# Attention tails of 64 queries as fp32 quarters of the array, in a fused retention, mixture-of-attention and token-mixing kernel

## The chip, the cores and the metric

One core of one Trainium2 chip runs the whole kernel. The metric is the device time of one execution in microseconds; lower is better. The time before the change is 927.81 us, the median of three runs (925.51 to 928.01).

## The reference

Three layers follow one another, on 8 batches of 576 positions. The first is a retention layer with 8 heads of 64. Its output x (512 wide) goes to four attention experts, and theirs to a token and channel mixing. The change touches the second layer only:

```python
logits = x @ w_gate                      # 4 experts, the best 2 count
topk = np.argpartition(-logits, K, axis=-1)[..., :K]
...
for e in range(E):
    q = x @ wq[e]
    k = x @ wk[e]
    v = x @ wv[e]
    scores = scale * (q @ k.transpose(0, 2, 1))
    scores = np.where(causal, -1000000000.0, scores)
    scores = scores - scores.max(-1, keepdims=True)
    a = np.exp(scores)
    a /= a.sum(-1, keepdims=True) + 1e-09
    ye = a @ v @ wo[e]
    for kk in range(K):
        mask = topk[:, :, kk] == e
        out += mask[..., None] * w[:, :, kk:kk + 1] * ye
```

All inputs and outputs are fp32.

## The kernel before, in words

**Attention units.** The 576 queries of a batch are four chunks of 128 and a tail of 64. The four experts are handled as two pairs (p = 0, 1). A unit (b, p, m) is query chunk m of one pair, for both experts of the pair (s = 0, 1). Its keys are those up to its own chunk; for the tail, m = 4, all 576. There are 80 units, of which 16 are tails.

**Precision.** Most products are made of operands split into a high and a low fp32r part (`split`, lines 102 and 103: a ScalarE copy and a VectorE subtraction), three matmuls each (`mm3`, lines 97 to 99). `proj_qk` makes Q and K of a pair that way, in two halves of 288 columns (g = 0, 1). For the scores, U holds Q's high and low part on the two halves of the partitions, and KK holds K's high part on both halves and K's low part on both halves; four DMAs per half of K, on SyncE's queue, copy KN into KK (line 225).

**One unit.** `at_scores` makes the scores in two matmuls per expert (line 309). VectorE adds the causal mask and takes the row minimum of the negated scores in one operation (line 312, two instructions: the operation and a read of its accumulator). ScalarE does the exponential with the row sum (line 317, again with a read of the accumulator). The tail's 576 keys don't fit one PSUM bank, so it has two parts of 288 and eight matmuls, and its second reduction starts from the first one's minimum. `at_trans` transposes P in blocks on TensorE with an identity (line 356); VectorE copies expert 0's blocks to PT and ScalarE expert 1's (lines 361 and 363). For the tail these are five blocks per expert, of 64 columns. `at_out` multiplies by V (line 375), for the query chunks (0), (1, 2) and (3, 4) together; key chunk 4 of V has 64 rows. `at_norm` turns the row sums of a pair into weights (lines 325 to 331).

**fp32 products** without a split (lines 132, 154, 161, 173 and 375) are two instructions each in the trace. Those of the retention scores (`ret_scores`, line 132) and its state (`ret_state`, line 173) use 64 rows and 64 columns, a quarter of the array.

**What sets the order.** TensorE's order is that of the program. VectorE, ScalarE and GpSimd take their instructions in an order that is made at build time, and each runs its queue in that order. At step t the program issues the scores of unit t, then projections by a table of slots, then the transposes of unit t-1, then retention work of the next batch and the products with V:

```python
SLOTS = [("Q01 K10", "R0"), ("", ""), ("K11 Q10", ""), ("Q11", "R1"), ("", "R2"),
         ("v0", "R3"), ("v1", ""), ("v2 k00", "R4"), ("q00", "R5"), ("v3 k01 v4 g", "")]
```

The first pair's tail is step 4 of a batch, between the retention steps R1 and R3. The second pair's is step 9, ahead of the projections v3, k01 and v4. Retention masks are VectorE's (lines 138 and 141), as are the gated outputs xt (line 181), which ScalarE and GpSimd split (lines 183 and 184). The last batch has no retention to do for a next one; token tiles fill its steps.

**Beside this**, about one job a step converts 64-bit weights to fp32r pairs (lines 434 to 455: SyncE loads, VectorE, ScalarE and GpSimd work), queued behind the step's reductions and exponentials (MARK). The PSUM pool has seven working banks ("w"), and P has five buffers.

## Time and profile before

| What | Value |
|---|---|
| Median of three runs | 927.81 us |
| Lowest and highest run | 925.51 and 928.01 us |
| The profiled execution, its own time | 925.94 us |
| Its span, from first to last instruction | 924.2 us |
| Mean granted TensorE clock | 0.991 |
| Matmul instructions | 8526 |

The span is what the trace shows; the 1.7 us beside it lie around the first and last instruction. Matmuls are pipelined, so the time from one start to the next is shorter than the duration of one, and a group of them is read by the start of what follows. PE is TensorE's matmul, PEld its weight load, DVE VectorE, ACT ScalarE, POOL GpSimd, SP SyncE.

### The profile page before, as it was taken

The numbers are of one execution on the slowest core, as the hardware profiler recorded it, in microseconds if no ns is written. First come the engines' busy times: TensorE is split into PE (matmuls) and PEld (weight loads), VectorE is DVE, ScalarE is ACT, GpSimd is POOL, SyncE is SP. The second block draws the span as 40 slices with busy tenths as digits, with TensorE's granted clock in tenths as the row PEclk, the third lists the DMA queues.
The fourth block names the chain that finished last, engine by engine and source line by source line (L and its number), as shares of the span: only waits on it lengthen the run. The fifth ranks groups of instructions, "written<-read, shape, count | busy, mean of one in ns | idle before, by whom it ended". The sixth has DMA issues, their size and how long they took to land.

```text
span 924.2 us, 22725 instructions
## 1 busy us (share of the span) xinstructions
PE 887.6 (96%) x8526; PEld 817.3 (88%) x8526; DVE 661.9 (72%) x2003; ACT 440.4 (48%) x1166; POOL 223.8 (24%) x276
## 2 busy tenths in 40 slices
PE   7899989999999999999999899999999999999998
PEld 6788978888888888888878899999999999999998
DVE  6487776877879787787777976766668674777632
ACT  2265645556556555555666533434334432444320
POOL 4316153361534525243121102102020110101010
PEclk8999999999999999999999899999999999999999
DMA  8667665776666776655685442343513333151311
GB/s 308 198 165 211 174 182 159 199 211 177 197 185 176 230 192 198 166 163 141 192 276 192 126 93 65 70 115 87 145 33 76 90 79 90 27 135 24 92 34 52
DMA packets 146205, 132.27 MB, mean 143 GB/s; under 512 B 83376, under 2 KB 121648, under 8 KB 146096
## 3 DMA queue, kind: packets, MB, share of 16 engines
q1 hardware_dynamic: 145952, 130.55, 50.5%
q8 instruction: 67, 1.10, 0.5%
q0 software_dynamic: 144, 0.28, 0.2%
q14 instruction: 42, 0.34, 0.1%
HBM read 80.20 MB, written 32.00 MB: 121 GB/s over the span
## 4 chain that ended last, share of the span: by engine, by line
PE 55%; DVE 7%; DMA 4%; ACT 3%; issue 2%; SPq 1%; POOL 1%; ACTq 0%; DVEq 0%; POOLq 0%
PE acc L712 22%; PE w L97 8%; PE w L99 8%; PE w L98 8%; PE w L375 3%; PE w L247 2%; PE w L309 2%; DMA KK<-KN 1%; ACT P L317 1%; DVE sm L138 1%; PE w L356 1%; DMA wost<-wot 1%; DMA og<-gd 1%; PE w L132 1%; DVE cs L577 1%
## 5 line engine op out<-in xcount | busy, mean ns | idle before, releaser
L712 PE MATMUL acc<-TK,zh 128*128 128x256 f32 (+1 forms) x1024 | 181.4, 300 | 3.9 <-DVE u L726 3.2
L712 PEld LDWEIGHTS acc<-TK,zh 128*128 128x128 f32 x1024 | 156.2, 192 | 4.5 <-ACT cs L575 3.4
L317 ACT ACTIVATE P<-P,st 128x128 f32<-128x128 f32 (+4 forms) x160 | 95.7, 600 | 68.0 <-DVE st L312 67.6
L712 PE MATMUL acc<-TK,zl 128*128 128x256 f32 (+1 forms) x512 | 110.7, 298 | 0.0
L728 POOL TENSOR_TENSOR ul<-u,uh 128x576 fp32r<-128x576 f32 x16 | 24.3, 1541 | 324.2 <-ACT uh L727 237.0
L712 PEld LDWEIGHTS acc<-TK,zl 128*128 128x128 f32 x512 | 87.4, 192 | 0.0
L102 ACT ACTIVATE zh<-cs 128x512 fp32r<-128x512 f32 x64 | 40.3, 631 | 90.1 <-PE acc L712 70.6
L375 PE MATMUL w<-PT,V 128*64 128x192 f32 (+3 forms) x576 | 67.1, 329 | 14.5 <-DVE PT L361 8.1
L97 PE MATMUL w<-xh,WH 128*128 128x288 f32 x256 | 76.6, 299 | 2.9 <-DVE sm L141 2.6
L103 DVE TENSOR_TENSOR zl<-cs,zh 128x512 fp32r<-128x512 f32 x64 | 44.9, 706 | 48.0 <-ACT zh L102 46.4
L309 PE MATMUL w<-KK,U 128*64 128x288 f32 (+4 forms) x384 | 77.8, 329 | 0.9 <-DMA KK<-KN 0.9
L575 ACT ACTIVATE cs<-cs 128x512 f32<-128x512 f32 x72 | 45.1, 631 | 67.4 <-DVE cs L573 54.0
L98 PE MATMUL w<-ul,CH 128*128 128x256 f32 (+1 forms) x256 | 75.7, 296 | 0.0
L375 PEld LDWEIGHTS w<-PT,V 128*64 128x64 f32 (+1 forms) x576 | 43.0, 138 | 36.9 <-ACT PT L361 13.2
L99 PE MATMUL w<-uh,CH 128*128 128x256 f32 (+1 forms) x256 | 75.7, 296 | 0.0
L97 PE MATMUL w<-uh,CH 128*128 128x256 f32 (+1 forms) x256 | 75.5, 297 | 0.1
L98 PE MATMUL w<-xl,WH 128*128 128x288 f32 x256 | 75.3, 294 | 0.0
L99 PE MATMUL w<-xh,WL 128*128 128x288 f32 x256 | 75.3, 294 | 0.0
L312 DVE CUSTOM_DVE_ANT_0 P<-w,cm 128x128 f32<-128x128 f32 (+4 forms) x160 | 72.2, 476 | 1.8 <-PE w L309 1.3
L138 DVE TENSOR_TENSOR sm<-w,tri 64x128 f32<-64x128 f32 x160 | 45.4, 284 | 25.5 <-PE w L132 17.7
L451 POOL TENSOR_TENSOR r<-r,ex 128x192 f32<-128x192 f32 (+1 forms) x51 | 29.5, 578 | 140.3 <-ACT P L317 52.0
L577 DVE SCALAR_TENSOR_TENSOR cs<-cs,x 128x512 f32<-128x512 f32 x72 | 48.8, 688 | 18.8 <-ACT cs L575 18.3
(142 smaller groups left out, 2192.5 us busy)
## 6 DMA issues: line engine op xcount, KB each, us to landing
kv<-kv SPq DMA_DIRECT2D x40, 512.0 KB
KK<-KN SPq DMA_DIRECT2D x128, 144.0 KB
kt<-qk SPq DMA_DIRECT2D x32, 512.0 KB
raw<-wd SPq DMA_DIRECT2D x43, 192.0 KB
xd<-xb SPq DMA_DIRECT2D x126, 64.0 KB
out<-u SPq DMA_DIRECT2D x28, 288.0 KB
u<-xd SPq DMA_DIRECT2D x28, 288.0 KB
td<-hl SPq DMA_DIRECT2D x27, 192.0 KB
```

The costliest lines, as they stand in the source:

```text
L97: nc.tensor.matmul(ps, ah, bh, start=first, stop=False)
L98: nc.tensor.matmul(ps, ah, bl, start=False, stop=False)
L99: nc.tensor.matmul(ps, al, bh, start=False, stop=last)
L103: nc.vector.tensor_sub(l, src, h)
L138: nc.vector.tensor_mul(sm[s][g, :, e, :64], ps[s][g, :, e, :64], tri[g, 2, None, :].to_broadcast([64, 2, 64]))
L309: nc.tensor.matmul(ps[s][:R], U[:, s, rs], KK[:, s, x, j0:j1], start=x == 0, stop=x == 1)
L312: MARK["dve"] = nc.vector.tensor_tensor_reduce(Ps[s][:R, j0:j1], ps[s][:R], cm[:R, o + j0:o + j1], 1.0, st[:R, 0, s:s + 1] if i else 3.0e3 ...
L317: MARK["act"] = nc.scalar.activation(Ps[s][:R, :n], Ps[s][:R, :n], AF.Exp, bias=st[:R, last, s:s + 1], scale=-1.0, accum_out=SUM[p][:R, m, ...
L375: nc.tensor.matmul(po[s * 64:s * 64 + 64, c0:], V[:ROWS[j], j, 2 * p + s, :], v, start=j == 0, stop=j == last, skip_group_check=True)
L575: nc.scalar.activation(cs, cs, AF.Sin)
L577: nc.vector.scalar_tensor_tensor(z, cs, -1.0, x2[:, None, ds].to_broadcast([128, 2, 256]), op0=OP.mult, op1=OP.mult)
L712: nc.tensor.matmul(acc[d][j], A[:, dc], TK[:, kt, W, t0:t1], start=q == 0 and n == 0, stop=q == 8 and n == 2)
```

## The change

- The tail's scores no longer use the split operands. `proj_qk` also keeps K of the pair as plain fp32 (K4, a ScalarE copy per half) and the last 64 queries as Q4. U, KK and KN shrink from 576 to 512 columns, so the second halves have 224 columns in place of 288.
- A new function `at_tail` makes the tail's scores as four fp32 products per pair: expert s on partition half s of K4 and Q4, keys 0 to 255 on output partitions 0 to 63, keys 256 to 575 on output partitions 64 to 127. P's tail is then 128 partitions by 320 columns. GpSimd fills the 64 columns that the lower half doesn't have. Each expert has a reduction over 256 columns and one over 64; three small VectorE operations join the minima of the two halves, and two more, after the exponentials, join the sums.
- The tail's transposes are three whole 128x128 blocks per expert, and PT is filled by copies with other patterns.
- V's tail stands on partitions 64 to 127, over rows that are set to zero once, so that the tail's product uses all 128 rows. V is two fixed tiles now.

```diff
@@ -90,6 +90,7 @@
     WL = w1p.tile([128, 4, NW1], F32R, name="WL")
     gt = ret.tile([128, 4, S], F32, name="gt")
     SB = [ret.tile([128, 4, D], F32, name=f"S{i}") for i in range(2)]
+    VS = [att.tile([128, NCH, E, D], F32, name=f"V{i}") for i in range(2)]
 
     SMT = [[ret.tile([128, 2, 2, 128], F32, name=f"sm{i}{q}") for q in range(2)] for i in range(2)]
 
@@ -210,32 +211,38 @@
     def proj_qk(b, p, t, g):
         xh, xl = XT[b]
         if (b, p) not in QKP:
-            QKP[b, p] = (atk.tile([128, 2, S], F32R, name="U", bufs=2), atk.tile([128, 2, 2, S], F32R, name="KK", bufs=2),
-                         atk.tile([128, 2, S], F32R, name="KN", bufs=2))
-        U, KK, KN = QKP[b, p]
+            QKP[b, p] = (atk.tile([128, 2, 512], F32R, name="U", bufs=2), atk.tile([128, 2, 2, 512], F32R, name="KK", bufs=2),
+                         atk.tile([128, 2, 512], F32R, name="KN", bufs=2),
+                         atk.tile([128, 64], F32, name="Q4", bufs=2), atk.tile([128, S], F32, name="K4", bufs=2))
+        U, KK, KN, Q4, K4 = QKP[b, p]
         w0 = (2 * p + t) * 128
         sl = slice(g * HS, g * HS + HS)
         ps = ps1.tile([128, HS], F32, name="w", bufs=WB, padded_shape=[128, 512])
         for kt in range(4):
             mm3(ps, WH[:, kt, w0:w0 + 128], WL[:, kt, w0:w0 + 128], xh[:, kt, sl], xl[:, kt, sl], kt == 0, kt == 3)
+        n = 512 - HS if g else HS
+        s2 = slice(g * HS, g * HS + n)
         if t:
-            split(KN[:, 0, sl], KN[:, 1, sl], ps)
+            split(KN[:, 0, s2], KN[:, 1, s2], ps[:, :n])
             for s in range(2):
                 for o in range(2):
-                    nc.sync.dma_start(KK[o * 64:o * 64 + 64, s, :, sl].bitcast(F32),
-                                      KN[s * 64:s * 64 + 64, :, sl].bitcast(F32))
+                    nc.sync.dma_start(KK[o * 64:o * 64 + 64, s, :, s2].bitcast(F32),
+                                      KN[s * 64:s * 64 + 64, :, s2].bitcast(F32))
+            nc.scalar.copy(K4[:, sl], ps)
             return
         for s in range(2):
             i, o = slice(s * 64, s * 64 + 64), slice(64 - s * 64, 128 - s * 64)
-            nc.scalar.activation(U[i, s, sl], ps[i], AF.Copy, scale=-0.125)
+            nc.scalar.activation(U[i, s, s2], ps[i, :n], AF.Copy, scale=-0.125)
         for s in range(2):
             i, o = slice(s * 64, s * 64 + 64), slice(64 - s * 64, 128 - s * 64)
-            nc.vector.scalar_tensor_tensor(U[o, s, sl], ps[i], -0.125, U[i, s, sl], op0=OP.mult, op1=OP.subtract)
+            nc.vector.scalar_tensor_tensor(U[o, s, s2], ps[i, :n], -0.125, U[i, s, s2], op0=OP.mult, op1=OP.subtract)
+        if g:
+            nc.scalar.activation(Q4, ps[:, n:], AF.Copy, scale=-0.125)
 
     def proj_v(b, c):
         xh, xl = XT[b]
         if c == 0:
-            VB[b] = att.tile([128, NCH, E, D], F32, name="V", bufs=2)
+            VB[b] = VS[b % 2]
         V = VB[b]
         l = LG[b % 2]
         w0 = 512
@@ -247,7 +254,7 @@
                 nc.tensor.matmul(ps[:R], x[:, kt, cs], W[:, kt, w0:w0 + NV], start=x is xh and W is WH and kt == 0,
                                  stop=x is xl and kt == 3)
         pv = ps[:R, :E * D].rearrange("p (e d) -> p e d", e=E)
-        nc.scalar.copy(V[:R, c, :, :], pv)
+        nc.scalar.copy(V[128 - R:, c, :, :], pv)
         nc.scalar.activation(l[:R, c, :], ps[:R, E * D:], AF.Copy)
 
     def gate(b):
@@ -295,13 +302,16 @@
 
     def at_scores(u):
         b, p, m = u
-        U, KK, _ = QKP[b, p]
+        U, KK, _, Q4, K4 = QKP[b, p]
+        if m == NCH - 1:
+            at_tail(u, Q4, K4)
+            return
         R = ROWS[m]
-        n = min(C * (m + 1), S)
+        n = C * (m + 1)
         rs = slice(m * C, m * C + R)
         st = att.tile([128, 2, 2], F32, name="st", bufs=3)
-        parts = [(0, n)] if n <= 512 else [(0, HS), (HS, S)]
-        Ps = [att.tile([128, S], F32, name="P", bufs=PB_N) for _ in range(2)]
+        parts = [(0, n)]
+        Ps = [att.tile([128, 512], F32, name="P", bufs=PB_N) for _ in range(2)]
         for i, (j0, j1) in enumerate(parts):
             ps = [ps1.tile([128, j1 - j0], F32, name="w", bufs=WB, padded_shape=[128, 512]) for _ in range(2)]
             for s in range(2):
@@ -318,6 +328,34 @@
                                  accum_out=SUM[p][:R, m, s:s + 1])
         PB[u] = Ps
 
+    def at_tail(u, Q4, K4):
+
+        p = u[1]
+        ps = [ps1.tile([128, 320], F32, name="w", bufs=WB, padded_shape=[128, 512]) for _ in range(2)]
+        for g, (j0, j1) in enumerate(((0, 256), (256, S))):
+            for s in range(2):
+                r = slice(s * 64, s * 64 + 64)
+                nc.tensor.matmul(ps[s][g * 64:g * 64 + 64, :j1 - j0], Q4[r, :], K4[r, j0:j1], start=True, stop=True,
+                                 skip_group_check=True)
+        st = att.tile([128, 5, 2], F32, name="st4", bufs=2)
+        lo, hi = slice(0, 64), slice(64, 128)
+        Ps = [att.tile([128, 512], F32, name="P", bufs=PB_N) for _ in range(2)]
+        for s in range(2):
+            nc.gpsimd.memset(Ps[s][lo, 256:320], 2.0 ** 30)
+            nc.vector.tensor_tensor_reduce(Ps[s][:, :256], ps[s][:, :256], cm[:, :256], 1.0, 3.0e38, OP.add, OP.min,
+                                           st[:, 0, s:s + 1])
+            nc.vector.tensor_tensor_reduce(Ps[s][hi, 256:320], ps[s][hi, 256:320], cm[hi, 576:640], 1.0, st[hi, 0, s:s + 1],
+                                           OP.add, OP.min, st[hi, 1, s:s + 1])
+        nc.vector.tensor_copy(st[lo, 1, :], st[hi, 1, :])
+        nc.vector.tensor_tensor(st[lo, 2, :], st[lo, 0, :], st[lo, 1, :], op=OP.min)
+        MARK["dve"] = nc.vector.tensor_copy(st[hi, 2, :], st[lo, 2, :])
+        for s in range(2):
+            MARK["act"] = nc.scalar.activation(Ps[s][:, :320], Ps[s][:, :320], AF.Exp, bias=st[:, 2, s:s + 1], scale=-1.0,
+                                               accum_out=st[:, 3, s:s + 1])
+        nc.vector.tensor_copy(st[lo, 4, :], st[hi, 3, :])
+        nc.vector.tensor_add(SUM[p][lo, NCH - 1, :], st[lo, 3, :], st[lo, 4, :])
+        PB[u] = Ps
+
     def at_norm(b, p):
 
         x = SUM[p]
@@ -336,8 +374,8 @@
         W = sum(ROWS[m] for m in ms)
         full = ms[0] + 1 if len(ms) == 1 else ms[1]
         if j < full:
-            return PT[:ROWS[j], j * W:(j + 1) * W], 0
-        return PT[:ROWS[j], full * W:full * W + ROWS[j]], W - ROWS[j]
+            return PT[:, j * W:(j + 1) * W], 0
+        return PT[:, full * W:full * W + ROWS[j]], W - ROWS[j]
 
     def at_trans(u):
         b, p, m = u
@@ -350,17 +388,24 @@
         W = sum(ROWS[x] for x in GROUPS[g])
         for s in range(2):
             PT = PTB[b, p, g][s]
-            tp = ps1.tile([128, m + 1, R], F32, name="w", bufs=WB, padded_shape=[128, 4, 128] if R == 128 else [128, 8, 64])
+            copy = nc.vector.tensor_copy if s in PTV else nc.scalar.copy
+            if m == NCH - 1:
+                tp = ps1.tile([128, 3, C], F32, name="w", bufs=WB, padded_shape=[128, 4, C])
+                for j, c0 in enumerate((0, C, 192)):
+                    nc.tensor.transpose(tp[:, j, :], Ps[s][:, c0:c0 + C], ident)
+                copy(PT[:, :4 * W].rearrange("q (a j w) -> q j a w", a=2, j=2)[:, :, :, off:],
+                     tp[:, :2, :].rearrange("q j (a c) -> q j a c", a=2))
+                copy(pt_view(PT, g, m)[0], tp[:, 2, 64:])
+                continue
+            tp = ps1.tile([128, m + 1, R], F32, name="w", bufs=WB, padded_shape=[128, 4, 128])
             for j in range(m + 1):
-                w = ROWS[j]
-                nc.tensor.transpose(tp[:w, j, :], Ps[s][:R, j * C:j * C + w], ident[:R, :R])
+                nc.tensor.transpose(tp[:, j, :], Ps[s][:, j * C:j * C + C], ident)
             n = min(m + 1, 4)
-            if off and m < 4:
+            if off:
                 n = m
-            copy = nc.vector.tensor_copy if s in PTV else nc.scalar.copy
             copy(PT[:, :n * W].rearrange("p (j w) -> p j w", j=n)[:, :, off:off + R], tp[:, :n, :])
             if n <= m:
-                copy(pt_view(PT, g, m)[0], tp[:ROWS[m], m, :])
+                copy(pt_view(PT, g, m)[0], tp[:, m, :])
 
     def at_out(b, p, g):
         V = VB[b]
@@ -372,7 +417,7 @@
         for j in range(last + 1):
             for s in range(2):
                 v, c0 = pt_view(PTs[s], g, j)
-                nc.tensor.matmul(po[s * 64:s * 64 + 64, c0:], V[:ROWS[j], j, 2 * p + s, :], v,
+                nc.tensor.matmul(po[s * 64:s * 64 + 64, c0:], V[:, j, 2 * p + s, :], v,
                                  start=j == 0, stop=j == last, skip_group_check=True)
         if g == 0:
             OB[b, p] = att.tile([128, S], F32, name="ob", bufs=2)
@@ -399,6 +444,8 @@
         nc.gpsimd.memset(l, 0.0)
     for x in SUM + NW:
         nc.gpsimd.memset(x, 1.0)
+    for i in range(2):
+        nc.gpsimd.memset(VS[i][:64, NCH - 1, :, :], 0.0)
     loads(0, 0)
     nc.sync.dma_start(tri, cst[:, 256:448].rearrange("p (a q) -> p a q", a=3))
     loads(0, 1)
```

## Rows read from the trace of the kernel before

**Rows 1.** Page, part 1: busy us (share of the span) and instructions, by engine

```profile
PE 887.6 (96%) x8526; PEld 817.3 (88%) x8526; DVE 661.9 (72%) x2003; ACT 440.4 (48%) x1166; POOL 223.8 (24%) x276
```

**Rows 2.** Waits, whole span: who <- for whom, us in total, times, longest

```profile
DVE nw L325 <- ACT P L317: 4.2, 6, 1.3
...
PE w L375 <- DVE PT L361: 8.1, 14, 3.0
...
PE w L375 <- ACT PT L361: 6.4, 12, 0.7
```

**Rows 3.** Timeline, VectorE, a first pair's tail: start us, us, what [idle before]

```profile
233.33 0.59 DVE L138 TENSOR_TENSOR sm<-w,tri 64x128 f32<-64x128 f32 x2 [0.97 <-PE w L132]
...
235.21 0.44 DVE L312 CUSTOM_DVE_ANT_0 P<-w,cm 64x288 f32<-64x288 f32 x1
...
236.84 0.68 DVE L361 COPY PT<-w 128x512 f32<-128x512 f32 x1
...
241.83 0.28 DVE L312 CUSTOM_DVE_ANT_0 P<-w,cm 128x128 f32<-128x128 f32 x1
...
242.25 0.41 DVE L361 COPY PT<-w 128x256 f32<-128x256 f32 x1
```

**Rows 4.** Timeline, TensorE, the same tail's products with V

```profile
242.72 0.54 PE L375 MATMUL w<-PT,V 128*64 128x192 f32 x2 [0.30 <-DVE PT L361]
243.46 1.72 PE L375 MATMUL w<-PT,V 128*64 128x192 f32 x16 [0.20 <-ACT PT L361]
244.92 0.33 PE L173 MATMUL w<-kt,S 64*64 64x128 f32 x2
245.01 0.23 PE L375 MATMUL w<-PT,V 64*64 64x64 f32 x2
```

**Rows 5.** Timeline, TensorE, a second pair's tail: scores and next block

```profile
205.98 1.26 PE L309 MATMUL w<-KK,U 128*64 128x288 f32 x8
207.09 0.65 PE L247 MATMUL w<-WH,xh 128*128 128x260 f32 x4
```

**Rows 6.** Timeline, TensorE: fp32 products in quarters, and next block

```profile
236.77 0.67 PE L173 MATMUL w<-kt,S 64*64 64x128 f32 x16
237.26 0.85 PE L132 MATMUL w<-kt 64*64 64x128 f32 x32
```

**Rows 7.** Timeline, TensorE: transposes of a tail and of chunk 2

```profile
215.89 0.29 PE L99 MATMUL w<-xh,WL 128*128 128x288 f32 x1
216.12 0.82 PE L356 MATMUL w<-ident,P 64*128 64x64 f32 x10
...
228.08 0.30 PE L99 MATMUL w<-xh,WL 128*128 128x288 f32 x1
228.21 0.82 PE L356 MATMUL w<-ident,P 128*128 128x128 f32 x6
228.96 0.69 PE L154 MATMUL pS<-vp,kv 128*64 128x64 f32 x16
```

**Rows 8.** Timeline, VectorE: small operations, each needing the last

```profile
214.55 0.17 DVE L271 TENSOR_REDUCE gmx<-gex 128x5 f32<-128x20 f32 x1
214.76 0.17 DVE L272 TENSOR_SCALAR gmx<-gmx 128x5 f32<-128x5 f32 x1
```

**Rows 9.** Groups by form: line, engine, operation, count | busy us, mean ns

```profile
L317 ACT ACTIVATE P<-P,st 128x384 f32<-128x384 f32 x32 | 19.5, 611 | 2.6 <-DVE st L312 2.3
...
L102 ACT ACTIVATE KN<-w 128x288 fp32r<-128x288 f32 x32 | 13.1, 408 | 7.8 <-PE w L99 7.2
...
L397 POOL MEMSET sm<- 64x128 f32 x8 | 1.6, 198 | 0.6 <-POOLq L874 0.3
```

**Rows 10.** Timeline: VectorE and TensorE at tail 2, TensorE in the last batch

```profile
128.40 0.49 DVE L442 TENSOR_SCALAR b<-raw 128x192 int32<-128x192 int32 x1 [2.57 <-POOL d L454]
...
129.46 3.03 PE L375 MATMUL w<-PT,V 128*64 128x192 f32 x18 [3.04 <-DVE PT L361]
...
465.59 0.41 PE L309 MATMUL w<-KK,U 128*128 128x128 f32 x2 [0.85 <-DMA KK<-KN]
```

## The prediction

> **What bounds the kernel now.** I read the page's busy shares first: TensorE is busy 96% of the span, VectorE 72%, ScalarE 48% [rows 1]. That makes TensorE time look like kernel time. So I read next what TensorE waits for: its two largest waits, 14.5 us in 26 pieces, fall on one line, L375, the product of P's transposes with V, and end with a PT copy of VectorE or ScalarE (L361) [rows 2]. Then I read the order of time around the tails (m = 4, 64 queries), of which there are 16. In batches 0 to 6 the two tails of a batch stand in different company, and the forecast rests on that. The second pair's tail (p = 1) lies among projections, long matmul blocks that TensorE does back to back; the first pair's tail (p = 0) lies among retention work, where VectorE is the late one.
>
> In the timeline of VectorE around a first-pair tail [rows 3] see the idle 0.97 us at 233.33 before the retention masks, and no wait of note from there to 242.25, where the tail's PT copy starts. TensorE gets its first two L375 at 242.72, after 0.30 idle, and the other sixteen only at 243.46, when ScalarE's copy is done too [rows 4]. ScalarE's copy stands behind the exponentials of the next unit, which wait for VectorE's reduction at 241.83. So here VectorE's queue since 233.33 sets the time; what TensorE saves between the masks and L375 becomes waiting.
>
> **The change part by part.**
>
> *Scores.* Eight fp32r matmuls of 64x288 (1.11 us from 205.98 to 207.09 [rows 5]) become four fp32 products, one in each 64x64 quarter of the array, of 256 or 320 columns. The trace shows no such product of that width. An fp32 product is two instructions here; the nearest row is L173: 16 instructions of 128 columns in 64x64 quarters, four in each, take 0.49 us until the next block [rows 6], 0.12 us per 128 columns in a quarter with all four running together. A whole-array fp32 transpose takes 0.109 us per 128 columns [rows 7]. The longest quarter streams 2 x 320 = 640 columns: 0.55 us by the second spacing, 0.61 by the first. One after another, the 2304 columns of all quarters would take 1.96 us. I take 0.58, because L173 is the nearest form: **0.53 us less** per tail. Going from quarters to full rows, TensorE stands for about 0.10 us, as before L356 at 216.12 (0.23 after the last L99, where 228.21 is 0.13 after its own [rows 7]). In batches 0 to 6 quarter work (L132 or L173) comes just ahead of the tail's scores, so one such switch is paid before and after the change alike. The last batch has none and pays two new ones.
>
> The Trainium skill ("TensorEngine Tiling (Array Packing)", Key Properties) says that changing the tiling mode drains TensorE. The 0.10 us above is what this trace shows of it; charged at both ends of all 16 tails it would add some 3 us, but 14 have a neighbour in the same mode.
>
> *Transposes.* Ten of 64 columns take 0.75 us with their exit; six of 128 columns take 0.75 us from 228.21 to 228.96 [rows 7]. Only the switch ahead of them goes: **0.10 us less**.
>
> *V's product.* The tail's four instructions now use all rows. Before, they ran in quarters beside the L173 that follows [rows 4]; after, they come ahead of the switch: between 0.1 us lost and 0.1 gained, I take 0.05 gained.
>
> *VectorE.* The four reductions take 1.63 us, 235.21 to 236.84 [rows 3]. After: two of 256 columns (at most 0.44 each, the 288 form) and two of 64 (at most 0.28 each, the 128-column form), each small one needing the sum just before it: 1.1 to 1.45 us. Then three tiny operations, each needing the one before: 0.21 us apart in the gate's chain [rows 8]. That is 1.7 to 2.1 us, so 0.1 to 0.45 more; I take 0.30. After the exponentials come two more tiny ones: 0.1 each between other work, 0.2 in a row; I take 0.30. Q's splits shrink by 64 of 288 columns, about 0.13 us per pair ahead of the tail. Sum: **0.47 more** per tail.
>
> *ScalarE.* Two exponentials of 576 columns become two of 320 (under the 0.61 us of 384 columns [rows 9]), but start only after both reductions; they end 0.1 to 0.4 later. K's fp32 copies are 32 of 0.41 us (the KN form [rows 9]) and Q's 16 shorter ones. ScalarE is idle half the time, so I cost them nothing; were that cover gone, one copy would delay a PT copy by 0.41. K's PSUM tile is held no longer, since VectorE's low part of K takes as long beside the new copy. SyncE issues the same number of K copies, half of them smaller.
>
> *GpSimd* gets two memsets per tail, under 0.2 us each [rows 9], early enough to be hidden; behind a product that waits for its load they would hold the exponentials.
>
> *The sum.* Second-pair tails of batches 0 to 6: 7 x (0.53 + 0.10 + 0.05) = **4.8 us less**, since TensorE does not wait there but for the copies that follow its own transposes. First-pair tails: what TensorE saves becomes waiting before L375, which comes later by VectorE's 0.47: 6 x 0.47 = **2.8 more**. The seventh, at 129.46, waits 3.04 us for a PT copy that stands on VectorE behind a weight conversion, itself held 2.57 us by GpSimd [rows 10]. I take it that GpSimd's work there follows TensorE's retention blocks and comes earlier with them: 0.6 less. Last batch: the scores save 0.53 less two switches, 0.33; at the first pair this is eaten by the wait for KK at 465.59 [rows 10], at the second it stays, and the transposes of both give 0.10 each: 0.5 less. Total: -4.8 + 2.8 - 0.6 - 0.5 = **-3.1 us**. The profiled execution took 925.9 us (span 924.2), 1.9 below the median of 927.8 of the runs shown; against the median the forecast is **924.7**.
>
> **The rivals.**
>
> *All of it arrives.* If VectorE's queue is laid out so that the tiny operations fall into its waits, the first-pair tails gain 0.68 too: 7 x 0.68 in place of the +2.2 net, -10.1 us, 917.7. For it: TensorE's 96%. Against: a wait of this kind stands before L375 in first-pair tails [rows 2, 4], with no idle VectorE ahead of it.
>
> *VectorE stands behind ScalarE (slower).* The copy of the upper half's sums (st, entry 3) waits for the second exponential. If it is queued right behind the three tiny operations, VectorE stands some 1.3 us, with the PT copy, xt and the next masks behind it. Then a first-pair tail costs 0.3 + 1.3 + 0.3 - 0.13 = 1.8: 6 x 1.8 - 5.9 = +4.9, 932.7. It decides from 1.0 us per tail on (6 x 1.0 pays back 5.9). For it: the norm's L325 already waits so, 4.2 us in 6 waits [rows 2]. Against: that is 0.7 a time, with other work put ahead.
>
> *Quarters in program order (slower).* If a quarter's first pass could start only after the second pass of the quarter ahead, the four would take 2 x 0.22 + 3 x 0.27 = 1.25 us; scores save nothing, the second pair gains nothing (0.14 lost against 0.15), and 2.8 us of VectorE stay: about 930.3. Against: the rows show L173's first two start at 244.92, before the second passes of the V product ahead of it in the program, at 245.01 [rows 4].
>
> The Trainium skill ("TensorE: Matmul & The Clock Gate", Part 3: Packing small matmuls) states that matmuls start and end in program order. By that rule the time is this rival's, 930.3; the row at 244.92 disagrees.
>
> **How the numbers follow.** Forecast 0.50 (921.5 to 927.8 by the bounds of VectorE's cost, 0.2 to 0.9 per tail, and of the quarters); all of it arrives 0.17; VectorE behind ScalarE 0.20; program order 0.08; the change not doing what it says (tails still in eight fp32r passes) 0, the diff excludes it; the remaining 0.05 is for a long wait like that at 129.46 won or lost by another order of the conversion work. About 0.3% (2.8 us) is what a measurement of this kernel can tell from no change. Of the forecast somewhat over half lies below 925.0; with the full gain, faster gets 0.48. The rest of the forecast and a little of the slower cases make no change 0.27; slower 0.25. Range 918 to 932.
>
> **What would show it.** Right: the second pair's scores near 0.6 us; no 0.1 us ahead of the transposes; VectorE's stretch from masks to the tail's PT copy longer by about 0.5 us; TensorE's wait before L375 in first-pair tails grown by about 1.1. Wrong: quarter starts 0.25 us apart (program order), no growth of that wait (full gain), or an idle VectorE ended by ScalarE's P of over 1 us (the slower rival).

## The result: 1.3% slower, and the profile after

The changed kernel takes 938.68 us (938.65 to 940.86 in four runs) against 927.86 (925.51 to 928.01) beside it: ratio 1.0128, 95% interval 1.0107 to 1.0150. The forecast was 924.7, its range 918 to 932. The profiled execution has a span of 936.9 us, 12.7 more than before.

The busy line of the page after, to be held against [rows 1]: TensorE does 3 us less, VectorE 16 us more.

```profile
PE 884.6 (94%) x8462; PEld 806.5 (86%) x8462; DVE 678.0 (72%) x2083; ACT 445.2 (48%) x1214; POOL 229.0 (24%) x310
```

What TensorE waits for, after (L420 is the product with V, L162 the retention product with the masked scores; before, see [rows 2]):

```profile
PE w L420 <- DVE PT L396: 8.3, 12, 2.3
PE w L162 <- DVE nw L365: 7.0, 4, 2.5
PE w L162 <- DVE sm L142: 6.0, 14, 0.7
PE w L420 <- ACT PT L406: 5.8, 8, 1.0
```

The second line is new: 7.0 us in four waits, before the retention product, which needs masks that now stand on VectorE among the norm's operations. (nw, the norm, is only what VectorE did just before.) The wait for VectorE ahead of the product with V, which the prediction saw growing, hardly did: 8.1 us [rows 2], now 8.3.

To see where the 12.7 us are, take the same TensorE instructions in both traces: the first product of each retention state (L154 before, L155 after), and at the end that of the last V projection. From one to the next, the growth of the difference belongs to that stretch. Summed over the stretches that hold the first pair's tails (numbered 1 to 7, batches 0 to 6) and those that hold the second pair's:

| us against before | forecast | after | single tails, after |
|---|---|---|---|
| first pair's tails | +2.2 | +12.9 | 4.3, -0.1, 2.6, 4.1, 2.5, 0.2, -0.6 |
| second pair's tails | -4.8 | -0.2 | -0.5, -0.2, 0.0, 0.0, 0.4, 0.5, -0.5 |
| ahead of them | 0 | +0.8 | |
| behind them | -0.5 | -0.9 | |

So both halves failed: the second pair's gain is missing, and the first pair costs six times its price, 11.0 us of it at tails 1, 3 and 4. At these three alone one of the two joining operations (L355, L356) took long: 1.22, 1.03 and 1.02 us, against 0.14 to 0.17 at the other four. Tail 5's loss has another start: a conversion that took 0.26 us before takes 1.21 at 301.02, while GpSimd makes xl, and stands ahead of the masks; 1.1 us of the 2.5 are lost there.

**A first pair's tail that lost 4.1 us (tail 4).** VectorE after, the tail of [rows 3], L139 and L142 being the masks, L355 and L356 the join of the sums, L490 and L494 conversions:

```profile
242.40 0.41 DVE L345 CUSTOM_DVE_ANT_0 P<-w,cm 128x256 f32<-128x256 f32 x1
...
243.74 0.69 DVE L406 COPY PT<-w 128x512 f32<-128x512 f32 x1
...
245.93 0.35 DVE L490 SCALAR_TENSOR_TENSOR b<-raw,b 128x192 int32<-128x192 int32 x1
246.31 1.02 DVE L355 COPY st<-st 64x2 f32<-64x2 f32 x1
247.36 1.39 DVE L494 SCALAR_TENSOR_TENSOR b<-ex,b 128x192 f32<-128x192 int32 x1
248.67 0.14 DVE L356 TENSOR_TENSOR sum<-st 64x2 f32<-64x2 f32 x1
248.74 0.27 DVE L139 TENSOR_TENSOR sm<-w,tri 64x128 f32<-64x128 f32 x1
248.94 0.15 DVE L363 TENSOR_SCALAR nw<-sum 128x10 f32<-128x10 f32 x1
249.13 0.29 DVE L139 TENSOR_TENSOR sm<-w,tri 64x128 f32<-64x128 f32 x1
...
251.78 0.42 DVE L396 COPY PT<-w 128x256 f32<-128x256 f32 x1
```

GpSimd in the same stretch:

```profile
246.26 1.04 POOL L118 TENSOR_TENSOR vp<-kv,gam 128x512 f32<-128x512 f32 x1 [3.47 <-DMA kv<-kv]
247.26 1.27 POOL L185 TENSOR_TENSOR xl<-xt,xh 128x512 fp32r<-128x512 f32 x1
```

From the first reduction to the PT copy it was 7.04 us before (235.21 to 242.25 [rows 3]) and is 9.38 now. The copy L355 of two columns takes 1.02 us and ends with GpSimd's product of vp; L494 takes 1.39 instead of about 0.36 and ends 0.2 us after xl; only then come the masks. At the tails where the copy meets neither product it takes 0.16 or 0.17. Before, the masks already ran while GpSimd did the same two products (VectorE and GpSimd in the kernel before):

```profile
239.50 0.55 DVE L138 TENSOR_TENSOR sm<-w,tri 64x128 f32<-64x128 f32 x2
240.06 0.42 DVE L141 TENSOR_TENSOR sm<-w,tri 128x256 f32<-128x256 f32 x1
```

```profile
239.52 1.04 POOL L117 TENSOR_TENSOR vp<-kv,gam 128x512 f32<-128x512 f32 x1 [4.13 <-DMA kv<-kv]
240.52 1.27 POOL L184 TENSOR_TENSOR xl<-xt,xh 128x512 fp32r<-128x512 f32 x1
```

The masks take one operand from PSUM, and none of them was held: of the 86 that began beside vp or xl from 40 to 440 us, none took over 0.03 us longer than usual.

The Trainium skill ("SBUF — State Buffer", Who interferes with whom) says that VectorE shares one port pair with GpSimd as an exclusive lock, taken by copies in a two-port mode and by operations with two SBUF inputs, and not by operations with at most one SBUF input outside those modes. These rows agree: the copy and L494 were held, the masks were not.

TensorE there, and its clock, by stretches of 2 us (the third number from the end is the granted clock):

```profile
247.45 0.69 PE L155 MATMUL pS<-vp,kv 128*64 128x64 f32 x16
250.27 0.66 PE L162 MATMUL w<-sm,vp 128*64 128x128 f32 x8 [2.13 <-DVE nw L365]
251.42 0.66 PE L162 MATMUL w<-sm,vp 128*64 128x128 f32 x8 [0.49 <-DVE sm L142]
252.25 3.71 PE L420 MATMUL w<-PT,V 128*64 128x192 f32 x20 [0.17 <-DVE PT L396]
```

```profile
248.00:250.00 2.00, 0.14 (x6) 0.00 (x0) 1.91 (x7) 0.70 (x3) 1.12 (x2) 1.00 0.82 217
...
254.00:256.00 2.00, 2.00 (x18) 1.46 (x18) 0.80 (x3) 0.36 (x1) 0.99 (x2) 0.50 0.50 124
```

The wait is followed by products with V at clock 0.50, the 1.2 GHz level: 3.65 us from 252.25 to 255.90. At tail 5, where the clock stays at 1.00, the same twenty take 1.57:

```profile
312.22 1.64 PE L420 MATMUL w<-PT,V 128*64 128x192 f32 x20 [0.76 <-DVE PT L396]
313.79 0.67 PE L174 MATMUL w<-kt,S 64*64 64x128 f32 x16
```

So 2.1 of tail 4's 4.1 us are the clock's. That second bill comes at tails 1 to 4; before, only tail 2 had it, after its stall at 129.46.

**A second pair's tail that lost its gain (tail 5).** Before, TensorE, then VectorE:

```profile
328.10 0.82 PE L356 MATMUL w<-ident,P 64*128 64x64 f32 x10
329.24 0.70 PE L375 MATMUL w<-PT,V 128*64 128x192 f32 x5 [0.32 <-DVE PT L361]
```

```profile
327.80 0.92 DVE L233 SCALAR_TENSOR_TENSOR U<-w,U 64x288 fp32r<-64x288 f32 x2
328.76 0.43 DVE L361 COPY PT<-w 128x256 f32<-128x256 f32 x1
```

and after:

```profile
341.10 0.82 PE L395 MATMUL w<-ident,P 128*128 128x128 f32 x6
342.99 1.24 PE L420 MATMUL w<-PT,V 128*64 128x192 f32 x10 [1.07 <-DVE PT L396]
```

```profile
341.69 0.79 DVE L238 SCALAR_TENSOR_TENSOR U<-w,U 64x224 fp32r<-64x224 f32 x2
342.51 0.42 DVE L396 COPY PT<-w 128x256 f32<-128x256 f32 x1
```

Before, VectorE came from the gate's chain, the conversions and Q's splits to the PT copy 0.66 us after the transposes began: just in time. After, it comes 1.41 us after. TensorE is earlier, VectorE is not, and the wait before the product with V went from 0.32 to 1.07 us.

### The profile page after: what moved, and what is told of

Its sections match the earlier page's. It is cut to its first block, busy times and chain, and to the rows that moved or that the text cites. A ratio compares the mean times of both kernels' runs of the same rounds, so it can differ in the third digit from the quotient of the medians.

```text
span 936.9 us, 22777 instructions
## 1 busy us (share of the span) xinstructions
PE 884.6 (94%) x8462; PEld 806.5 (86%) x8462; DVE 678.0 (72%) x2083; ACT 445.2 (48%) x1214; POOL 229.0 (24%) x310
## 4 chain that ended last, share of the span: by engine, by line
PE 48%; DVE 2%; ACT 1%; DMA 1%; issue 1%; SPq 1%; POOL 0%; DVEq 0%; ACTq 0%; POOLq 0%
PE acc L759 25%; PE w L98 7%; PE w L99 7%; PE w L100 7%; DMA wost<-wot 1%; PE w L319 1%; PE w L420 1%; ACT P L327 0%; DVE cs L620 0%; DMA KK<-KN 0%; PE w L254 0%; PE w L402 0%; POOL ol L575 0%; PE acc L749 0%; SPq L574 0%
## 5 line engine op out<-in xcount | busy, mean ns | idle before, releaser
L327 ACT ACTIVATE P<-P,st 128x128 f32<-128x128 f32 (+3 forms) x128 | 71.1, 557 | 59.0 <-DVE st L322 58.1
L104 DVE TENSOR_TENSOR zl<-cs,zh 128x512 fp32r<-128x512 f32 x64 | 50.1, 783 | 49.6 <-ACT zh L103 48.9
L420 PE MATMUL w<-PT,V 128*64 128x192 f32 (+3 forms) x576 | 68.4, 341 | 16.4 <-DVE PT L396 8.3
L420 PEld LDWEIGHTS w<-PT,V 128*64 128x64 f32 x576 | 45.9, 146 | 37.5 <-DVE PT L396 11.5
L139 DVE TENSOR_TENSOR sm<-w,tri 64x128 f32<-64x128 f32 x160 | 45.6, 285 | 26.6 <-PE w L133 19.0
L322 DVE CUSTOM_DVE_ANT_0 P<-w,cm 128x128 f32<-128x128 f32 (+3 forms) x128 | 59.2, 484 | 2.4 <-PE w L319 1.8
L319 PE MATMUL w<-KK,U 128*128 128x128 f32 (+3 forms) x256 | 57.5, 343 | 0.7 <-DMA KK<-KN 0.3
```

The lines of the kernel that those rows point to most:

```text
L104: nc.vector.tensor_sub(l, src, h)
L139: nc.vector.tensor_mul(sm[s][g, :, e, :64], ps[s][g, :, e, :64], tri[g, 2, None, :].to_broadcast([64, 2, 64]))
L319: nc.tensor.matmul(ps[s][:R], U[:, s, rs], KK[:, s, x, j0:j1], start=x == 0, stop=x == 1)
L322: MARK["dve"] = nc.vector.tensor_tensor_reduce(Ps[s][:R, j0:j1], ps[s][:R], cm[:R, o + j0:o + j1], 1.0, st[:R, 0, s:s + 1] if i else 3.0e3 ...
L327: MARK["act"] = nc.scalar.activation(Ps[s][:R, :n], Ps[s][:R, :n], AF.Exp, bias=st[:R, last, s:s + 1], scale=-1.0, accum_out=SUM[p][:R, m, ...
L420: nc.tensor.matmul(po[s * 64:s * 64 + 64, c0:], V[:, j, 2 * p + s, :], v, start=j == 0, stop=j == last, skip_group_check=True)
```

## The experiments

The expectations number tails (or "batches") 1 to 7. Runs in one group shared their runs of the kernel before. "First" and "second" are the sums over the seven first and second pair's tails, as above.

**1. GpSimd's memsets.**

```
-  Ps = [att.tile([128, 512], F32, name="P", bufs=PB_N) ...]   # at_tail
+  Ps = [att.tile([128, 320], F32, name="P4", bufs=2) ...]     # PB_N 5 -> 4
```

> The changed kernel, but the tail's P has two buffers of its own (and the other units four), so that GpSimd's second memset of a tail no longer waits for the transposes of the units before. First theory (the two small VectorE operations behind the tail's exponentials, caught under GpSimd's products, delay the retention masks): those operations stay where they are, so about 938 us, 936 to 940. Second theory (the memsets hold GpSimd's queue by about 2 us per first-pair tail and push its products over VectorE's work): the loss goes, about 928 us or less.

942.93 us, ratio 1.0157 (1.0132 to 1.0182). GpSimd's wait for the transposes fell from 40.8 to 12.1 us and the time did not (first +10.6, second +2.4). The second theory falls, with one reserve: the other units have a buffer of P less here, whose cost was not measured by itself.

**2. The join left out.**

```
-  copy(st[lo, 4], st[hi, 3]); add(SUM[lo, 4], st[lo, 3], st[lo, 4])
+  accum_out=SUM[p][:, NCH - 1, s:s + 1]                       # of the exponentials
```

> The changed kernel without the copy and the addition that join the two halves' sums of exponentials (the tail's norm uses the sum over the first 256 keys alone; that part is left out). First theory: the masks of the first pair's tails come back to within about 0.5 us of their old place, the losses of 3 to 5 us at three of these tails go or shrink below 1 us; time 925 to 931, about 928 us. Second theory: the memsets and GpSimd's queue are unchanged, so about 938 us. Third theory (the other order of the conversion work or ScalarE's copies of K and Q cost the time): also about 938 us.

933.38, ratio 1.0076 (1.0048 to 1.0105); first +6.6, second -1.0. About half of the loss goes with the join; of the four stretches at clock 0.50 those at tails 1, 3 and 4 are gone, and one at tail 5 has come.

**3. Join and norm behind the next reductions.**

```
-  if units[t][2] == NCH - 1: at_norm(...)                     # join in at_tail
+  if units[t - 1][2] == NCH - 1:
+      with tc.issue_after(MARK["dve"].ins): at_norm(...)      # join and norm
```

> The changed kernel with the same work in another order: the join of the sums and the norm of a pair are issued on VectorE only behind the reductions of the next unit, so behind the retention masks. First theory: VectorE reaches the masks earlier than in the kernel before, which has the norm ahead of them; no first-pair tail loses over 1 us; 918 to 926, about 922 us. Second and third theory: about 938 us, at best 936 from the norm's own 0.8 us at some tails.

941.62, ratio 1.0145 (1.0130 to 1.0161): a miss. VectorE at tail 2, then TensorE:

```profile
127.23 0.84 DVE L364 COPY st<-st 64x2 f32<-64x2 f32 x1
130.12 0.26 DVE L493 TENSOR_SCALAR b<-raw 128x192 int32<-128x192 int32 x1 [2.05 <-POOL d L505]
...
130.87 0.41 DVE L400 COPY PT<-w 128x256 f32<-128x256 f32 x1
```

```profile
131.34 3.04 PE L424 MATMUL w<-PT,V 128*64 128x192 f32 x20 [3.75 <-DVE PT L400]
```

The masks come early, but now the join and a conversion that waits for GpSimd stand ahead of the PT copy. The same wait moved; it did not go.

**4. Quarters at the second pair alone.**

```
-  if m == NCH - 1:  at_tail(u, Q4, K4)
+  if m == NCH - 1 and p:  at_tail(u, Q4, K4)                  # p = 0 as before
```

> Only the second pair's tails in quarters; the first pair's tails with the eight fp32r products, four reductions and exponentials of 576 columns of the kernel before (their last transpose takes 128 columns, so that V's product uses all rows). All theories put the loss of the changed kernel at the first pair's tails, and the second pair's gain of 7 times about 0.55 to 0.68 us remains: about 924 us, 922 to 926. If the loss came from something that the second pair's tails bring with them (K's and Q's copies on ScalarE, GpSimd's memsets there): over 930.

930.48, ratio 1.0034 (1.0018 to 1.0051): neither. Second -1.9 instead of about -4, and the first pair's tails, whose work is nearly the old one, lost 5.9, 2.3 of it at the stall of tail 2, which grew.

**5. The join on ScalarE.**

```
-  nc.vector.tensor_copy(...); nc.vector.tensor_add(...)
+  nc.scalar.activation(..., AF.Copy); 2 x nc.scalar.activation(..., AF.Identity, bias=...)
```

> The changed kernel with the join of the two halves' sums on ScalarE (a copy and two additions by bias) instead of VectorE. First theory (about half of the loss is the join standing ahead of the masks on VectorE, as the run without a join showed with 933.4): the norm follows the join, so the masks come ahead of it; 931 to 935, about 933 us. If the loss is not VectorE's but comes from the join being waited for: 938.

936.63, ratio 1.0097 (1.0068 to 1.0126). Only 2 us: the norm still follows, among the masks. The first pair's sum fell to +8.8, and the work behind the tails took 2.7 us of that back.

**6. Two small operations in the kernel before.**

```
+  nc.vector.tensor_copy(du[:R, 0], SUM[p][:R, m]); nc.vector.tensor_add(du[:R, 1], ...)
```

> The kernel before with two small VectorE operations more behind each tail's exponentials (a copy and an addition of 64x2, whose result nobody reads). First theory: the two alone delay the masks of the first pair's tails, by 0.3 us where they run freely and by up to 2 where GpSimd's products catch them: 930 to 935, about 932 us. If small operations cost only their own time of 0.15 us and there is room for them: 928.

928.48, ratio 1.0014 (0.9995 to 1.0033). The first theory as I had put it falls: in the profiled execution the two cost 1.0 and 1.8 us at tails 1 and 2 and at most 0.4 at the others, and the median hardly moves. Alone they are not what costs 3 to 5 us.

**7, 8. Join, norm and conversions behind the PT copies, with and without the change.**

```
+  MARK["dve" if s in PTV else "act"] = copy(<the tail's last PT copy>)
+  with tc.issue_after(MARK["dve"].ins): at_norm(...)          # and the conversions
```

> The changed kernel with the join, the norm and the conversion work of that step issued on VectorE only behind the tail's PT copies. In the run with the join behind the next reductions (941.6) a conversion operation that waits for GpSimd stood ahead of the PT copy and cost 2 to 3.4 us at four tails. If that order is all: no first-pair tail loses over 1 us and the second pair's gain stands; 919 to 926, about 923 us. If the tail's own VectorE work (reductions, joins of the minima) already uses up what TensorE saves: 926 to 931, about 928. If the order does not matter: 938 or more.

932.17, ratio 1.0066 (1.0039 to 1.0092).

> The kernel before with the same order: the norm and the conversion work of that step behind the tail's PT copies. If the order is what the changed kernel lacks and the kernel before has by luck, only its stall of 3 us at 129.46 goes: 922 to 926, about 924 us. If the order costs elsewhere (GpSimd's conversions come later and hold their buffers longer): 928 to 932.

935.39, ratio 1.0089 (1.0066 to 1.0112). Same order, and the changed kernel is not the slower one: 3.2 us ahead by the medians, though the intervals overlap. Against each other the second pair's tails keep -3.1. What both lose is at the next step, where a conversion now stands ahead of the masks. In the kernel before it waits for its load:

```profile
351.48 0.66 DVE L444 TENSOR_SCALAR b<-raw 128x192 int32<-128x192 int32 x1 [3.14 <-DMA raw<-wd]
352.06 0.58 DVE L138 TENSOR_TENSOR sm<-w,tri 64x128 f32<-64x128 f32 x2
```

and in the changed kernel it is caught under xl (1.21 us instead of 0.26):

```profile
350.15 1.21 DVE L500 TENSOR_SCALAR ex<-b 128x192 int32<-128x192 int32 x1
351.28 0.58 DVE L139 TENSOR_TENSOR sm<-w,tri 64x128 f32<-64x128 f32 x2
```

**9 to 11. The order taken apart.** Only join and norm behind the PT copies; the same for the kernel before's norm; and the conversions too, at the second pair alone. (Diffs: the lines of 7, without the first; with it under `if p`.)

> The changed kernel with the join and the norm alone issued behind the tail's PT copies; the conversion work keeps its old marks. If the loss at the first pair's tails of batches 1, 3 and 4 (5.1, 3.0 and 4.5 us in the trace after) is the join and the norm among the masks, these three shrink to the 1 us or so that the tail's other VectorE work costs; the stall of batch 2 stays, and the second pair's tails still give back some of their gain to conversion operations ahead of the PT copies: 927 to 932, about 930 us. If the join itself is not what costs: 936 or more.

933.47, ratio 1.0074 (1.0053 to 1.0096). Tails 1 and 4 fell from 4.3 and 4.1 to 0.3 and 1.0; tail 3 stayed at 2.3, tails 2 and 7 rose to 2.0: conversions ahead of the PT copy.

> The kernel before with the norm behind the tail's PT copies and the conversion work where it was. In the run with both moved the kernel before lost 8 us, at the step after the tails, where conversion work that came late stood ahead of the next masks. If that was the conversions: 925 to 929, about 927 us. If it was the norm: 933 or more.

927.92, ratio 1.0009 (0.9997 to 1.0020). The norm's place is free in the kernel before.

> The join and the norm behind the tail's PT copies, and the conversion work behind them at the second pair's tails alone. With the conversions behind the copies everywhere (932.2) the second pair's tails kept their 0.55 us each, but late conversions held the masks of the next step by 1.6 to 2.1 us at three places and xl by 3.6 at one. If the second pair's gain comes from the conversions there and those losses from the first pair's: 923 to 928, about 926 us. If the losses come from the conversions of the second pair: 930 to 934.

940.73, ratio 1.0146 (1.0124 to 1.0167): a miss. The second pair kept -3.7, but the conversions came late and held the next masks (3.0 us lost at 122.06) and the PT copy of tail 7.

**12, 13. Without GpSimd's product vp, with and without the change.**

```
-  vp = ...; nc.gpsimd.tensor_mul(vp, u[:, 1, :]..., gam...)
+  vp = u[:, 1, :].rearrange("p (h d) -> p h d", h=H)
```

> The changed kernel without GpSimd's product of the values with gamma (vp; the values themselves are used, that factor is left out), so that about half of GpSimd's long products are gone. To be compared with the kernel before without the same product. If GpSimd's hold on VectorE is what makes the loss: at most 5 us more than that kernel, against 10.8 between the two kernels as they are. If it is the order of VectorE's queue alone: still some 10 us more.

932.77, ratio to the kernel before 1.0063 (1.0045 to 1.0081).

> The kernel before without GpSimd's product of the values with gamma (left out as in the other run). It has few operations under GpSimd's products near its tails: within 3 us of the kernel before, about 925 us, its stall of 3 us at 129.46 shorter.

920.66, ratio 0.9938 (0.9920 to 0.9956). Against my expectation the change costs 12.1 us here too, and vp costs each kernel about 6 us. The equal totals hide a shift, though: from one of these traces to the other the first pair's tails lose 7.8 us and not 12.9, none of them at clock 0.50; the second pair's sum is -0.1; and 3.2 us are now lost behind the tails, in the last batch, 2.3 of them in one wait for exponentials at 505.03. So vp does account for some 5 us at the first pair's tails, and that the total stayed is in part chance. With vp gone the two traces run evenly and show the rest. VectorE without the change:

```profile
176.75 0.44 DVE L310 CUSTOM_DVE_ANT_0 P<-w,cm 64x288 f32<-64x288 f32 x1
...
178.37 0.68 DVE L359 COPY PT<-w 128x512 f32<-128x512 f32 x1
...
183.46 0.42 DVE L359 COPY PT<-w 128x256 f32<-128x256 f32 x1
```

and with it:

```profile
178.21 0.41 DVE L343 CUSTOM_DVE_ANT_0 P<-w,cm 128x256 f32<-128x256 f32 x1
...
179.56 0.69 DVE L404 COPY PT<-w 128x512 f32<-128x512 f32 x1
180.16 0.15 DVE L347 COPY st<-st 64x2 f32<-64x2 f32 x1
180.35 0.15 DVE L348 TENSOR_TENSOR st<-st 64x2 f32<-64x2 f32 x1
180.54 0.16 DVE L349 COPY st<-st 64x2 f32<-64x2 f32 x1
...
185.76 0.42 DVE L394 COPY PT<-w 128x256 f32<-128x256 f32 x1
```

Reductions to PT copy: 6.71 us without, 7.55 with, 0.84 more. The reductions take 1.35 instead of 1.62; the three joins of the minima 0.57. The remaining 0.54 are the join of the sums and the gaps of the norm, whose operations now stand one by one among the masks: of the 0.84, 0.17 lie ahead of the first mask (181.03 and 182.66) and 0.67 behind it. Five of the seven tails lose 0.5 to 1.0 (0.8 on average). The two others lose 1.6 and 2.3, and there something was held under xl, here at tail 2 a part of the norm that takes 0.15 elsewhere:

```profile
125.27 1.24 DVE L361 TENSOR_SCALAR nw<-sum 128x10 f32<-128x10 f32 x1
126.43 0.27 DVE L137 TENSOR_TENSOR sm<-w,tri 64x128 f32<-64x128 f32 x1
```

Counted over the traces from 40 to 440 us, operations of VectorE that last over 0.25 us longer than the lower quartile of their line and form: before 21 with 10.7 us of excess, after 37 with 21.1; without vp 11 with 3.7 and 23 with 9.5. The change moved more of VectorE's work under GpSimd's, with vp and without it. Only half of these operations lie beside vp or xl (before 10 of 21, after 19 of 37); most of the others lie beside GpSimd's own steps of the conversions. A run without xl was not tried.

**14, 15. No conversions at the tails' steps.**

```
+  while jobs[i] and t % 5 not in (4, 0) and ...
```

> The changed kernel with no conversion work issued at the step of a tail's scores nor at the next one; the same work is issued in the other three steps. If the conversion work ahead of masks and PT copies is what turns the VectorE's half microsecond into long waits: no wait over 1.5 us at a first-pair tail, second-pair gains kept; 922 to 929, about 926 us, and no more than 2 us above the kernel before with the same schedule. If the join under GpSimd's products is enough for the loss: 932 to 938.

960.90, ratio 1.0372 (1.0349 to 1.0394).

> The kernel before with the same schedule of the conversion work. Its stall of 3 us at 129.46 goes; the conversions are denser in the other steps: 923 to 930, about 926 us. By the forecast's own sum the changed kernel should be some 2 to 6 us below it, since the second pair's tails keep their gain and no stall is lost or won.

952.92, ratio 1.0293 (1.0258 to 1.0328). Misses, and with this schedule the changed kernel is 8 us slower, where it should have been 2 to 6 faster. Two conversions in one step wait for GpSimd in between, ahead of the PT copies of the other steps; in the kernel before that wait rose from 8.1 us [rows 2] to

```profile
PE w L375 <- DVE PT L361: 20.8, 17, 2.7
```

**16 to 18. The even setting without the join, and in the other order.** All without vp; the edits are those of 2, 7 and 8.

> The changed kernel without vp's product (gamma left out) and without the join of the sums (the tail's norm uses the sum over 256 keys alone). Against the changed kernel without vp (932.8): the join's two operations and the gaps that they bring measured 0.33 us in that trace, so about 7 times 0.35, 930.3, 929 to 931.5. If the join costs more by where it stands (5.3 us with vp's product in place): 927 to 928.

925.04, ratio to the kernel before 0.9983 (0.9969 to 0.9997). The join costs 7.7 us here, more than either expectation had: 0.40 at each of six first pair's tails, near the 0.35 expected, 1.5 at tail 2, where the norm is no longer held, 0.9 at the second pair's tails; of the rest, 2.3 is the wait for exponentials in the last batch, which is gone.

> The changed kernel without vp's product, with the join, the norm and the conversions behind the tail's PT copies. The second pair's tails should keep their 0.55 us each and the first pair's tails lose the join and the norm ahead of the masks (0.33 us and some 0.3 us of gaps among them): 932.8 less 3.9 less 4, about 925 us, 921 to 929. If late conversions hold the next masks as they did with vp in place: 930 to 935.

929.02, ratio 1.0025 (1.0009 to 1.0041): at the upper end of the range. Against the kernel before without vp the second pair kept -3.8, but late conversions stood ahead of the masks again; tail 2 lost 3.3 us.

> The kernel before without vp's product in the same order. If the order costs the kernel before what it did with vp in place (8 us): about 928 us, above the changed kernel in this order. If that loss came from GpSimd's product: about 921 us, and the change still costs some us in this order too.

930.15, ratio 1.0031 (1.0014 to 1.0047). In this order the change costs nothing: second pair -3.9, first pair +2.5 against each other. The second pair's gain is there at all seven tails (-0.5 to -0.6 each). That the first pair's sum comes near the forecast's +2.2 is luck: at tail 2 alone it is made of -3.4 and +4.3 us in stretches that follow each other. And the order itself costs the kernel before 9.5 us (930.15 against 920.66), so nothing is won.

## Why the prediction was wrong, point by point

**The scores: right.** The stretch with the second pair's scores is 0.56 us shorter at all seven tails (0.53 forecast). Of this 0.45 is the product itself and 0.11 the switch ahead of it, which the prediction had read off the transposes at 216.12 [rows 7]; those go from full rows to 64, not from quarters to full rows. The quarters run together; the chain after, with L338 as the quarters:

```profile
212.56 0.46 PE L174 MATMUL w<-kt,S 64*64 64x64 f32 x16
212.84 0.72 PE L338 MATMUL w<-K,Q 64*64 64x256 f32 x8
213.49 0.39 PE L254 MATMUL w<-WH,xh 128*128 128x260 f32 x1
```

0.65 us with the exit. The four first passes start within 0.02 us of each other. The rival of program order (1.25 us) is out, and with it the rule that the prediction cites for it, as the rival had applied it; which order the passes have in the program the trace does not show. **Transposes: right**, 0.09 to 0.11 less at six of the first pair's tails (at tail 5 the stretch holds the wait for the masks). V's 0.05 is too small to be read.

**"TensorE does not wait there": the step that failed first.** The -4.8 us of the second pair came out as -0.2. I read the busy TensorE and long projections around those tails, and never looked whether VectorE arrives at the PT copy with time to spare. It had none. Runs 7, 11 and 17 show most of the gain (-3.0 to -3.8) once the conversions stand behind that copy.

**VectorE's 0.47 per first-pair tail: mis-sized, and incomplete.** Undisturbed it is 0.8. The first part, +0.30 for reductions and three joins, was right. The two operations behind the exponentials were priced at 0.30 and cost 0.54 with the norm that they push among the masks; the 0.13 that Q's splits save does not lie in that stretch. What was missing altogether is that a copy, an operation with a scalar or one with two inputs, all in SBUF, can be held on VectorE under GpSimd's vp and xl for 1 us, that the norm and the conversions behind it then slide as well, and that the waits of 2.1 to 2.5 us at tails 1, 3 and 4 were paid again at half the clock. That made 0.8 into 1.8 on average.

**Tail 2** gained 0.1 instead of 0.6: its stall went from VectorE's wait of 2.57 [rows 10] to one of 2.02, with other waits ahead of it. **ScalarE at nothing**: right but for one wait for K's fp32 copy, at 50.43 in the first batch, where TensorE loses 0.5 us. **GpSimd's memsets**: nothing in the runs speaks against the price of nothing (run 1, with its reserve).

**The rivals.** VectorE standing behind ScalarE came nearest in size (932.7), by the wrong mechanism: the join waited for the exponentials 0.03 to 0.08 us at five of the first pair's seven tails, and 0.5 at two. It did stand so at the second pair's tails 1 and 2 (1.3 us each, at 99.59 and 157.89), which lost little by it. The small remainder, 0.05 for another order of the conversion work, was the nearest in kind. That the same new order makes the changed kernel 6.5 us faster and the kernel before 7.9 us slower (runs 7 and 8) was in neither the range nor the chances.

What stays open: how the first pair's loss divides between xl's hold and the late norm over all tails; and no order was found in which the changed kernel beats the kernel before as it stands (with vp 932.17 at best against 927.46, without vp 929.02 against 920.66).

## What to carry to other kernels

Before TensorE time is booked as saved, look at when the next consumer of its output starts: a copy that begins 0.03 us after the operation ahead of it has no slack, and everything saved upstream becomes waiting. Tiny VectorE operations cost their place in the queue, not their 0.15 us: ask what is behind them, and which GpSimd product they may start under. Compare two versions with the same order of the side work as well as with the one that they happen to get, since the order alone was worth 6 to 8 us here, and the change 11.

## What the runs showed of the hardware

A VectorE copy of 64x2 elements took 0.16 us alone and 1.02 when it began under GpSimd's 128x512 product, and a 128x10 operation went from 0.15 to 1.24, while masks with an operand in PSUM ran beside the same products unchanged; the profile shows the hold as duration, not as a wait, so the list of waits never names it. Removing one of GpSimd's two products per chunk, 40 us of its busy time, made the kernel before 6 us faster, though GpSimd is idle three quarters of the span.
